# A mixture-of-experts kernel after an mLSTM: the second expert's matrices requested later, its first matrix cast and split later

## The chip, the cores and the metric

The kernel runs on one core of a Trainium2 chip. The metric is the device time of one execution in microseconds. The engines are called PE (TensorE, matrix products), ACT (ScalarE), DVE (VectorE), POOL (GpSimd) and SP (SyncE, which here only issues transfers). "SPq" is SP's sequencer. Transfers that SP issues share one queue on the 16 DMA engines; indirect transfers (gathers and scatters) are issued by POOL on another.

## The reference

The first stage is a recurrent attention with a matrix state for 4 sequences of 768 steps and 8 heads of 40; its result, scaled by a sigmoid gate, makes 3072 rows `x` of 320 numbers. The second stage is a mixture of 16 experts (4 groups of 4), and each row goes to one of them:

```python
g_idx = np.argmax(x @ w_group, axis=1)              # the group, g_w its softmax weight
e_idx = np.argmax(xg @ w_expert[g], axis=1)         # the expert in it, e_w its softmax weight
h = np.maximum(xg[mask_e] @ w1[g, e], 0.0)          # 320 -> 1024
ye = h @ w2[g, e]                                   # 1024 -> 320
out[tok_idx] = (g_w * e_w)[:, None] * ye
```

## The kernel before

The whole order of instructions is written out by hand; each engine runs its own in program order, and the framework puts in the waits. The first stage goes through 24 units (6 chunks of 128 steps, 4 sequences). While it runs, every unit's rows are stored in the DRAM tensor `x_d`, the rows' experts are found, and a table `itab` in DRAM takes, expert by expert, the number and weight of each row (scatters by POOL).

The experts then run in order of falling size, each with room for a fixed number of rows (384 in the first, 352 in the second, and so on down). An expert has these steps. Its index list `ix` is loaded from `itab`; POOL gathers its rows (`xg`, in blocks of 128) from `x_d` by that list; PE transposes them (line 778), and ACT and DVE make of them a high and a low half (`xhl`). Its matrices are loaded as `w1s` (1536 KB) and `w2s` (1280 KB); ACT casts each piece to a high half and DVE makes the low half, the difference (`w1h`, `w1l`, `wsk`, `w2h`, `w2l`; lines 728 and 732). PE makes the first products in four groups `psh` (line 758), ACT and DVE make of each a high and low relu (`hh`), and PE makes the second products `po` (lines 803 to 805). ACT scales these to `y`, which POOL scatters to the output (line 615).

The first expert is begun before all rows are known. Its first 256 rows (the early block, `early_expert`, lines 685 to 718) are gathered while the last units run. Its last 128 rows (the late block) are those that came from the last chunk: they don't go by the index list. POOL scatters the last chunk's rows straight into a small DRAM tensor `x_l` (`put_places`, line 513), and SP loads this as `xg` (line 1311); the load must wait for all scatters. PE transposes the rows in `early_turn` (line 675), called in the middle of the early block's second group of 128 rows, between its sixth and seventh of eight filter rows. The late block is narrow: its groups hold 256 columns (high and low together), and ACT copies a part `hs` (line 863) and DVE adds the rest (line 864) before the relu.

The order around the change:

- `last_units` (line 995) ends the first stage. After the last store it issues, on SP, a tiny transfer `peek` that waits for the early gathers (line 1113), and then `do(early_loads)` (line 1114). `early_loads` holds what is left of the requests for the first two experts' matrices: at this place the second expert's four, two halves of `w1s` and two of `w2s` (`load_tasks`, line 624).
- `lists` (line 1307) is a generator whose pieces run between the early block's groups of first products. Its first piece puts the last rows into `x_l`, requests the load of `x_l` on SP, scatters the last rows' numbers to `itab`, and requests on SP the late rows' list `li` (line 985) and the second expert's `ix` (line 644). `li` waits for the scatters into `itab`. The next piece requests the third expert's list and lets POOL gather the second expert's rows (`load_x`, line 611).
- `early_expert` calls `after()` between its first and its second products. Before the change this is `second_w1`, which casts and splits the second expert's `w1` (three casts on ACT, three differences on DVE).
- `expert((0, 1), ...)` (line 1340) runs the late block. Its argument `own` is a list of casts; after each of the four groups of first products one of them is taken, cast and split. Before the change the list is empty. In the middle of the late block's second products PE transposes the second expert's rows (`turn2`, through `mid`, line 799).
- The second expert then runs in the loop from line 1344, with the casts of its `w2` as `own`.

Of the kernel before, what the change touches and what calls it, by code (L numbers as in the profile page):

```python
# [42 lines left out]
NEARLY, NPICK, EARLY, LATE = 1, 2, 256, 128  # L43
CAPS = [EARLY + LATE, 352, 320, 288, 256, 256, 256, 256, 192, 192, 192, 192, 160, 160, 160, 128]
# [12 lines left out]
def lstm_moe(ctx: ExitStack, tc: tile.TileContext, gates, qkT, nat, og, wcat, w1, w2, cst, out):  # L57
# [38 lines left out]
    ps_1 = first_banks.enter_context(tc.tile_pool(name="ps_1", bufs=1, space=PSUM))  # L96
# [21 lines left out]
    rt = {}  # L118
# [370 lines left out]
    def put_id():  # L489
        if ids:  # L490
            sl, tk = ids.pop(0)
            nc.gpsimd.memset(sep, 0.0)
            no_order("ids", nc.gpsimd.indirect_dma_start(
                out=itab_flat, out_offset=bass.IndirectOffsetOnAxis(ap=sl, axis=0), in_=tk, in_offset=None))


    def put_ids():
        while ids:
            put_id()
# [118 lines left out]
    ereg, w1st, w2st, ixs, wsp_, xhls = {}, {}, {}, {}, {}, {}  # L618
# [66 lines left out]
    def early_expert(W, ws, idx, lists, after, last):  # L685
        w1h, w1l, wsk, w2h, w2l = (ws[n] for n in ("w1h", "w1l", "wsk", "w2h", "w2l"))
        xhl = xhls[0, 0]
        hh = pools["hp"].tile([P, NF, 2 * W], F32R, name="hh")
        xh, xl = [xhl[:, k, 0, :] for k in range(3)], [xhl[:, k, 1, :] for k in range(3)]
        for f in range(0, NF, 2):  # L690
            ps = pools["ps_h"].tile([P, 512], F32, name="psh")
            for g in range(2):
                s0 = slice((f + g) * P, (f + g + 1) * P)
                s1 = slice(F + (f + g) * P, F + (f + g + 1) * P)
                todo = [(w1h, s0, xh[0]), (w1h, s0, xl[0]), (w1h, s1, xh[1]), (w1h, s1, xl[1]), (wsk, s0, xh[2]),
                        (wsk, s0, xl[2]), (w1l, s0, xh[0]), (w1l, s1, xh[1])]
                for n, (w, s, x) in enumerate(todo):
                    mm(ps[:, g * W:(g + 1) * W], w[:, s], x, start=(n == 0), stop=(n == len(todo) - 1))
            if f == 0:
                steps(lists)  # L700
            a, hr = ps.rearrange("p (q w) -> p q w", q=2), hh[:, f:f + 2, 0:W]
            nc.scalar.activation(hr, a, AF.Relu)
            nc.vector.scalar_tensor_tensor(hh[:, f:f + 2, W:], a, 0.0, hr.bitcast(F32), op0=ALU.max, op1=ALU.subtract)
            steps(lists)
        after()
        for i, m in enumerate(blocks(W)):
            t, tl = slice(i * P, i * P + m), slice(W + i * P, W + i * P + m)
            po = pools["ps_o"].tile([P, DM], F32, name="po")
            for f in range(NF):
                s = slice(f * DM, (f + 1) * DM)  # L710
                if f == NF - 2 and i == len(blocks(W)) - 1:
                    do(last())
                mm(po, hh[:, f, t], w2h[:, s], start=(f == 0), stop=False)
                mm(po, hh[:, f, t], w2l[:, s], start=False, stop=False)
                mm(po, hh[:, f, tl], w2h[:, s], start=False, stop=(f == NF - 1))
            y = pools["hp"].tile([P, DM], F32, name="y", bufs=3)
            nc.scalar.activation(y, po, AF.Copy, scale=idx(i, m)[:, 1:2].bitcast(F32))
            no_order("out", scatter(y, idx(i, m)[:, 0:1]))
# [197 lines left out]
    def do(tasks, n=99):  # L916
        while tasks and n:
            tasks.pop(0)()
            n -= 1

    def ix_of(r):
        return lambda i, m: ixs[r][0:m, i, :]

    xgs, early_loads, early_splits = {}, [], []
# [54 lines left out]
    def steps(g, n=1):  # L979
        for _ in range(n):  # L980
            next(g, None)
# [13 lines left out]
    def last_units():  # L995
        a, b, c, d = range(HAND, NU)
        loads(d)
        decays(c, "upper")
        put_ids()
        decays(d, "upper")  # L1000
        scores(a)
        norm(a - 1)
        norm1(a - 1)
        norm2(a - 1)
        norm3(a - 1, "reciprocal")
        masked(a, 0)
        norm3(a - 1, "mult")
        masked(a, 1)
        carried(a)
        rows(a - 1)  # L1010
        logits(a - 2)
        carried2(a)
        turn(a - 1)
        r1 = turned_logits(NCH - 2)
        steps(r1, 2)
        values(a)
        steps(r1, 4)
        decays(c, "exp")
        steps(r1)
        logits(a - 1)  # L1020
        r2 = route(NCH - 2, B - 1, B, rt["bank"])
        steps(r1, 2)
        norm(a)
        steps(r1)
        norm1(a)
        steps(r1)
        norm2(a)
        steps(r1)
        norm3(a, "reciprocal")
        steps(r1, 4)  # L1030
        put_ids()

        scores(b)
        steps(r2)
        steps(r1)
        steps(r2)
        steps(r1)
        steps(r2, 2)
        masked(b, 0)
        steps(r2, 2)  # L1040
        masked(b, 1)
        carried(b)
        steps(r2)
        decays(d, "exp")
        steps(r2)
        norm3(a, "mult")
        steps(r2)
        carried2(b)
        steps(r2, 2)
        rows(a)  # L1050
        steps(r2, 6)
        put_ids()
        load_ix(0, nc.gpsimd)
        xgs[0] = load_x(EARLY, ix_of(0), True)
        steps(r2, 2)
        steps(early_counts(), 9)
        values(b)

        turn(a)
        late_first()  # L1060
        do(early_splits, 2)
        scores(c)
        norm(b)
        norm1(b)
        norm2(b)
        norm3(b, "reciprocal")
        masked(c, 0)
        norm3(b, "mult")
        masked(c, 1)
        logits(a)  # L1070
        carried(c)
        rows(b)
        carried2(c)
        values(c)
        do(early_splits)
        do(lows, 2)

        turn(b)
        scores(d)
        norm(c)  # L1080
        norm1(c)
        norm2(c)
        norm3(c, "reciprocal")
        masked(d, 0)
        norm3(c, "mult")
        masked(d, 1)
        logits(b)
        r3 = route(NCH - 1, 0, 2, rt["bank"])
        carried(d)
        steps(r3, 2)  # L1090
        rows(c)
        steps(r3, 3)
        carried2(d)
        steps(r3)
        values(d)
        steps(r3)
        busy(1)
        turn(c)
        busy(2)
        norm(d)  # L1100
        steps(r3)
        norm1(d)
        steps(r3)
        norm2(d)
        steps(r3)
        norm3(d, "reciprocal")
        steps(r3)
        norm3(d, "mult")
        steps(r3)
        rows(d)  # L1110
        logits(c)
        turn(d)
        nc.sync.dma_start(peek, xgs[0][-1][0:1, 0:2])
        do(early_loads)
        xl = early_turn((0, 0), EARLY, xgs[0], ((ps_a, "it"), (ps_s, "sp")))
        steps(r3, 9)
        put_rows()
        put_ids()
        put_places(late_p, xgs["late"])
        do(lows, 1)  # L1120
        do(xl)
        logits(d)
        busy(4)
        rt["r4"] = route(NCH - 1, 2, B, rt["bank"])
        steps(rt["r4"], 6)
# [29 lines left out]
    with tc.manual_schedule():  # L1155
# [106 lines left out]
        tp = gate_cols(1, NCH)  # L1262
# [40 lines left out]
        own, rest = casts(1)  # L1303
# [3 lines left out]
        def lists():  # L1307
            steps(rt["r4"], 12)
            put_rows()
            xgs[0, 1] = [mxp.tile([P, ROW], F32, name="xg", bufs=8)]  # L1310
            nc.sync.dma_start(xgs[0, 1][0][0:LATE], x_l)
            put_ids()
            li = late_list()
            rt["late"] = lambda i, m: li[0:m]
            load_ix(1)
            yield
            next(experts)
            load_e(2, [ET.SP, ET.Pool])
            load_ix(2)
            xgs[1] = load_x(CAPS[1], ix_of(1))  # L1320
            yield
            do(lows, 1)
            yield
            do(lows, 2)
            yield

        def second_w1():
            for act, low in own:
                act()
                low()  # L1330

        early_expert(EARLY, wsp_[0], ix_of(0), lists(), second_w1, lambda: early_turn((0, 1), LATE, xgs[0, 1], [(ps_1, "tp")]))
        load_w1(2, nc.gpsimd)
        load_w2(2, nc.gpsimd)
        early_banks.close()
# [1 line left out]
        pools["ps_h"] = enter(tc.tile_pool(name="ps_h2", bufs=3, space=PSUM, reuse_waits="tile"))  # L1337
        pools["ps_o"] = enter(tc.tile_pool(name="ps_o2", bufs=2, space=PSUM, reuse_waits="tile"))
        pools["late"] = True
        expert((0, 1), LATE, rt["late"], [], (), lambda: turn2(1, CAPS[1], xgs[1]))  # L1340
        own = rest
        next(experts, None)
        xgs[2] = load_x(CAPS[2], ix_of(2))
        for r in range(NEARLY, NE):
# [12 lines left out]
            own = list(rest)  # L1357
# [3 lines left out]
    with tc.For_i(0, nv, 1):  # L1361
# [31 lines left out]
        tp = pools["ps_h"].tile([P, 2, 512], F32, name="psh")[:, 0, 0:3 * P].rearrange("p (k w) -> p k w", k=3)  # L1393
# [83 lines left out]
```

## Time and profile before

| | us |
|---|---|
| median of 3 runs | 434.77 |
| lowest and highest | 433.32, 435.80 |
| the profiled execution | 429.81 |
| its span in the trace | 427.8 |
| PE busy | 393.3 (92% of the span) |
| DVE busy | 326.5 (76%) |
| ACT busy | 273.4 (64%) |
| POOL busy | 194.6 (45%) |
| DMA, mean over the span | 221 GB/s |

A busy engine is one that executes; register, branch and DMA-issuing instructions don't count. In a timeline each line is start, duration (both in us), engine, line of the kernel, operation, output and inputs, count, and in brackets how long the engine was idle before and what ended that. In a list of waits the numbers are the total, the count and the longest. In the chain of waits each line is start, duration and what the end was waiting for at that time. In windows the columns are the stretch, its length, the busy time of PE, of PE's weight load, DVE, ACT and POOL, then the clock granted to PE as a share of full speed, the share of time in which the DMA engines were busy, and GB/s. `psh`, `po` and the like are the program's tiles; `a<-b,c` is an instruction that writes a and reads b and c.

### The profile page before, as it was taken

What the parts mean: (1) busy time and instruction counts of PE and PEld (TensorE: products, weight loads), DVE (VectorE), ACT (ScalarE), POOL (GpSimd) and SP (SyncE); (2) the same over time, 40 slices, a digit from 0 to 9 for tenths busy, and PEclk for the clock granted to TensorE, in tenths of its full rate; (3) what the DMA queues carried; (4) which work ended last, traced back from release to release, by engine and by line L of the source; (5) the groups of instructions that cost most, each with busy time, mean ns of one, the idle gap of its engine ahead of it and who ended that gap; (6) DMA issues with size and microseconds to landing.
All of it is one profiled execution on the core that took longest, in us unless ns stands there. A gap on an engine that the chain in (4) does not pass through costs nothing.

```text
span 427.8 us, 9374 instructions
## 1 busy us (share of the span) xinstructions
PE 393.3 (92%) x3341; PEld 374.2 (87%) x3341; DVE 326.5 (76%) x738; ACT 273.4 (64%) x607; POOL 194.6 (45%) x220
## 2 busy tenths in 40 slices
PE   8888999897988898979999999999999999999960
PEld 5878989887977797969999999999999999999960
DVE  5787898989879899747837465666669999999940
ACT  3858677585778733444745466567468888888840
POOL 6656576774857626546231322422422334442210
PEclk9999999999999999999999999999999999999995
DMA  6969998998999616639864657657665877676000
GB/s 186 296 181 329 314 314 255 268 280 230 311 332 308 160 40 180 197 83 338 314 220 133 216 199 254 202 188 276 209 227 211 317 264 246 229 274 243 2 25 1
DMA packets 30518, 94.73 MB, mean 221 GB/s; under 512 B 9600, under 2 KB 13953, under 8 KB 26886
## 3 DMA queue, kind: packets, MB, share of 16 engines
q1 hardware_dynamic: 25094, 79.48, 57.8%
q0 software_dynamic: 5104, 14.28, 9.6%
q8 instruction: 27, 0.44, 0.4%
q10 hardware_dynamic: 272, 0.36, 0.3%
q14 instruction: 21, 0.17, 0.2%
HBM read 83.84 MB, written 12.00 MB: 224 GB/s over the span
## 4 chain that ended last, share of the span: by engine, by line
PE 58%; DVE 11%; DMA 10%; ACT 8%; issue 6%; POOL 4%; POOLq 0%; SPq 0%; DVEq 0%; ACTq 0%
PE psh L758 24%; PE po L803 6%; PE po L804 6%; PE po L805 6%; ACT ab L191 3%; PE psh L778 2%; DMA x_d<-x 2%; PE po L809 2%; PE sp L201 2%; PE po L808 2%; PE av L277 2%; DMA ab<-a_d 2%; DVE pt L207 2%; DMA qk<-in_qkT_dram 1%; PE busy L125 1%
## 5 line engine op out<-in xcount | busy, mean ns | idle before, releaser
L615 POOL DMA_INDIRECT out_dram<-y,ix x34 | 44.9, 1320 | 132.8 <-ACT y L817 115.4
L758 PE MATMUL psh<-xhl,w1h 128*128 128x256 f32 (+4 forms) x368 | 85.8, 309 | 0.4 <-DVE xhl L678 0.3
L758 PEld LDWEIGHTS psh<-xhl,w1h 128*128 128x128 f32 x368 | 59.9, 189 | 1.0 <-DVE xhl L678 0.5
L803 PE MATMUL po<-w2h,hh 128*128 128x320 f32 (+1 forms) x192 | 60.7, 316 | 0.0
L804 PE MATMUL po<-w2l,hh 128*128 128x320 f32 (+1 forms) x192 | 59.3, 309 | 0.0
L805 PE MATMUL po<-w2h,hh 128*128 128x320 f32 (+1 forms) x192 | 59.2, 308 | 0.0
L191 ACT ACTIVATE ab<-ab,bcol 128x128 f32<-128x128 f32 x176 | 53.8, 388 | 4.5 <-POOL ab L158 2.9
L732 DVE TENSOR_TENSOR w2l<-w2s,w2h 128x640 fp32r<-128x640 f32 x64 | 51.8, 824 | 6.3 <-ACT w2h L728 5.3
L277 PE MATMUL av<-nt,pt 128*128 128x128 f32 x384 | 49.4, 282 | 1.9 <-DVE pt L207 1.9
L758 PE MATMUL psh<-xhl,w1l 128*128 128x256 f32 (+6 forms) x256 | 49.1, 273 | 0.0
L277 PEld LDWEIGHTS av<-nt,pt 128*128 128x128 f32 x384 | 45.0, 192 | 3.3 <-DVE pt L207 1.7
L201 PE MATMUL sp<-qk 128*128 128x128 f32 x384 | 47.0, 276 | 0.0
L758 PE MATMUL psh<-xhl,wsk 128*128 128x256 f32 (+4 forms) x184 | 46.8, 304 | 0.0
L853 DVE SCALAR_TENSOR_TENSOR hh<-psh,hh 128x512 fp32r<-128x512 f32 (+3 forms) x36 | 21.5, 615 | 32.2 <-ACT hh L850 32.0
L611 POOL DMA_INDIRECT xg<-x_d,ix x34 | 35.8, 1053 | 21.6 <-DMA ix<-itab 11.3
L728 ACT CAST w2h<-w2s 128x640 fp32r<-128x640 f32 x64 | 44.9, 723 | 0.0
L201 PEld LDWEIGHTS sp<-qk 128*128 128x128 f32 x384 | 44.8, 192 | 0.2
L732 DVE TENSOR_TENSOR w1l<-w1s,w1h 128x1024 fp32r<-128x1024 f32 x32 | 38.9, 1219 | 6.4 <-ACT w1h L728 6.2
L758 PEld LDWEIGHTS psh<-xhl,w1l 128*128 128x128 f32 x256 | 42.4, 188 | 0.0
L850 ACT ACTIVATE hh<-psh 128x512 fp32r<-128x512 f32 (+3 forms) x28 | 18.0, 644 | 31.9 <-PE psh L758 31.9
L207 DVE TENSOR_TENSOR pt<-sp,ab 128x512 f32<-128x512 f32 x48 | 32.7, 683 | 4.7 <-PE sp L201 2.8
L803 PEld LDWEIGHTS po<-w2h,hh 128*128 128x128 f32 (+1 forms) x192 | 35.8, 187 | 0.5
(200 smaller groups left out, 872.7 us busy)
## 6 DMA issues: line engine op xcount, KB each, us to landing
w1s<-in_w_dram SPq DMA_DIRECT2D x12, 1536.0 KB
w2s<-in_w_dram SPq DMA_DIRECT2D x13, 1280.0 KB
ab<-a_d SPq DMA_DIRECT2D x22, 512.0 KB
nt<-in_nat_dram SPq DMA_DIRECT2D x24, 324.0 KB
qk<-in_qkT_dram SPq DMA_DIRECT2D x48, 160.0 KB
x_d<-x SPq DMA_DIRECT2D x23, 192.0 KB
sig<-in_og_dram SPq DMA_DIRECT2D x6, 640.0 KB
w1s<-in_w_dram SPq DMA_DIRECT2D x4, 768.0 KB
```

Of the source, the lines that this page charges most:

```text
L191: nc.scalar.activation(ab[:, j, :], ab[:, j, :], AF.Exp, bias=bcol[:, c, b * H + j:b * H + j + 1])
L201: mm(sp[:, jj, :], qk[:, j % 2, j // 2, :], qk[:, 2, j // 2, :], start=True, stop=True)
L207: nc.vector.tensor_tensor(pt, t["pm"][hh], t["ab"][:, 4 * hh:4 * hh + 4, :], op=ALU.mult)
L277: mm(t["av"][:, o:o + P], t["pm"][hh][:, jj, :], nt[:, o:o + P], start=True, stop=True)
L611: return nc.gpsimd.indirect_dma_start(out=o, out_offset=None, in_=src, in_offset=bass.IndirectOffsetOnAxis(ap=idx, axis=0))
L615: return nc.gpsimd.indirect_dma_start(out=out, out_offset=bass.IndirectOffsetOnAxis(ap=idx, axis=0), in_=y, in_offset=None, bounds_check=N ...
L728: nc.scalar.copy(t[names[0]][:, dst], src[r][:, s])
L732: nc.vector.tensor_tensor(o, src[r][rows, s], h.bitcast(F32), op=ALU.subtract)
L758: mm(ps[:, g, 0:n_], w[:, s], x, start=(n == 0), stop=(n == len(todo) - 1))
L803: mm(po[0:m], hh[:, f, t], w2h[:, s], start=st0, stop=False)
L804: mm(po[0:m], hh[:, f, t], w2l[:, s], start=False, stop=False)
L805: mm(po[0:m], hh[:, f, tl], w2h[:, s], start=False, stop=sp0)
```

## The change

The second expert's four requests go from the end of the first stage to the first piece of `lists`, right behind the request for the load of `x_l` and ahead of those for `li` and `ix`, on the same queue. `early_expert` gets nothing to do between its products, and the late block gets the three casts and splits as `own`: the first three of its four groups are each followed by one.

```diff
@@ last_units
         turn(d)
         nc.sync.dma_start(peek, xgs[0][-1][0:1, 0:2])
-        do(early_loads)
         xl = early_turn((0, 0), EARLY, xgs[0], ((ps_a, "it"), (ps_s, "sp")))
@@ lists
             put_rows()
             xgs[0, 1] = [mxp.tile([P, ROW], F32, name="xg", bufs=8)]
             nc.sync.dma_start(xgs[0, 1][0][0:LATE], x_l)
+            do(early_loads)
             put_ids()
             li = late_list()
             rt["late"] = lambda i, m: li[0:m]
             load_ix(1)
@@
-        def second_w1():
-            for act, low in own:
-                act()
-                low()
-
-        early_expert(EARLY, wsp_[0], ix_of(0), lists(), second_w1, lambda: early_turn((0, 1), LATE, xgs[0, 1], [(ps_1, "tp")]))
+        early_expert(EARLY, wsp_[0], ix_of(0), lists(), lambda: None, lambda: early_turn((0, 1), LATE, xgs[0, 1], [(ps_1, "tp")]))
         load_w1(2, nc.gpsimd)
         load_w2(2, nc.gpsimd)
@@
-        expert((0, 1), LATE, rt["late"], [], (), lambda: turn2(1, CAPS[1], xgs[1]))
+        expert((0, 1), LATE, rt["late"], list(own), (), lambda: turn2(1, CAPS[1], xgs[1]))
         own = rest
```

## The prediction

> **What bounds the kernel now.** I read the page first, then the waits of the tensor engine (PE), the chain of waits around the one large wait, and then the engines' timelines there.
>
> ```profile
> span 427.8 us, 9374 instructions
> ```
>
> The waits of PE over the whole span, and those after 196 us (in total, times, longest):
>
> ```profile
> PE tpm L675 <- DMA xg<-x_l: 2.6, 1, 2.6
> ...
> PE psh L758 <- DVE xhl L786: 0.2, 1, 0.2
> ```
>
> The first is the largest single wait of PE for a transfer in the span: it wants the late block's rows, `xg<-x_l`. The second is all that PE waits for between 196 and 412 us. So from the second expert on, PE is the bound, and whatever makes that expert start later or earlier moves the end by as much. The change has to be judged by one number: when the second expert's first products can run.
>
> The chain of waits from 174 to 187 us:
>
> ```profile
> 174.66 4.47 DMA x_l<-pt,place
> ...
> 179.15 5.68 DMA xg<-x_l
> ...
> 184.87 0.56 PE tpm L675 x3
> ...
> 186.58 0.45 PE psh L758 x2
> ```
>
> The last scatter into `x_l` lands at 174.66 + 4.47 = 179.13, its load takes 5.68 more, and PE transposes at 184.87. PE's timeline beside it:
>
> ```profile
> 181.93 0.31 PE L715 MATMUL po<-w2h,hh 128*128 128x320 f32 x1
> ...
> 193.04 1.07 PE L778 MATMUL psh<-cs,xg 128*128 128x128 f32 x9
> ...
> 196.22 0.75 PE L758 MATMUL psh<-xhl,w1h 128*128 128x352 f32 x3 [0.17 <-DVE xhl L786]
> ```
>
> PE runs out of work at 182.24 and stands for 2.63 us. The late block's products begin at 186.58 (T below); at 193.04, which is T + 6.46, stand the transposes of the second expert's rows, and 3.18 later, at 196.22, its products run without gaps. **The most that the change can win is that stall of 2.63 us, 0.6% of the run.**
>
> **The part that is moved: four requests on SP's queue.** SP's timeline:
>
> ```profile
> 166.49 0.90 SPq L629 DMA_DIRECT2D w1s<-in_w_dram  x2
> ...
> 167.57 1.41 SPq L629 DMA_DIRECT2D w2s<-in_w_dram  x2
> ...
> 179.15 0.33 SPq L1311 DMA_DIRECT2D xg<-x_l  x1
> 183.06 0.33 SPq L985 DMA_DIRECT2D li<-itab  x1
> 183.58 2.37 SPq L644 DMA_DIRECT2D ix<-itab  x3
> ```
>
> The matrices (two halves of w1 of 768 KB, two of w2 of 640 KB, 2.88 MB) are issued from 166.49 to 168.98. Moved behind the load at 179.15, they have nothing before them on SP but that load. Behind them come `li` and the index lists `ix`. SP is done with four requests 2.5 us after it starts, before `li` may go (it waits for the last scatter into `itab`), so SP itself holds up nothing. The queue of the transfers does.
>
> **What it wins: scatters.** The gather queue's timeline (POOL):
>
> ```profile
> 172.06 1.00 POOL L513 DMA_INDIRECT x_l<-xg,late_p  x1 [0.30 <-issue]
> ...
> 176.55 1.00 POOL L493 DMA_INDIRECT itab<-tokw,slot  x1 [0.25 <-issue]
> ...
> 186.24 0.97 POOL L611 DMA_INDIRECT xg<-x_d,ix  x1 [7.43 <-DMA ix<-itab]
> ...
> 188.78 0.93 POOL L611 DMA_INDIRECT xg<-x_d,ix  x1 [0.30 <-issue]
> ```
>
> And the time from issue to landing of three of these, those at 172.06, 176.55 and 188.78, in this order:
>
> ```profile
> DMA to landing us min/median/max: 6.7/6.7/6.7
> ...
> DMA to landing us min/median/max: 3.0/3.0/3.0
> ...
> DMA to landing us min/median/max: 3.2/3.2/3.2
> ```
>
> DMA in windows of one microsecond (the last two columns are the share of the 16 engines and GB/s):
>
> ```profile
> 174.00:175.00 1.00, 1.00 (x11) 1.00 (x10) 1.00 (x3) 0.60 (x1) 0.70 (x2) 1.00 1.02 412
> ...
> 176.00:177.00 1.00, 1.00 (x9) 1.00 (x8) 0.97 (x2) 0.60 (x1) 0.75 (x3) 1.00 0.31 109
> ```
>
> The matrices keep the engines full at 412 GB/s and are through at about 176.5, 10.0 us after the first request. A scatter beside them takes 6.7, one just behind them 3.0. POOL issues its scatters 1.3 apart whatever the DMA does, so the last still goes out at 174.66; with 3.0 in place of 4.47 it lands at 177.7, 1.45 earlier (bounds: 0 and 1.45). The load's 5.68 was taken with the engines almost idle; I leave it (bounds from the landings above: 3.2, as a gather of 128 such rows takes, to 6.7). Rows land at 183.4; PE stands 1.2 instead of 2.63, and T becomes 185.1.
>
> **What it costs: the index lists of the second expert.** The place in the queue matters, and a later part of the trace shows it. SP, then POOL:
>
> ```profile
> 349.39 0.33 SPq L629 DMA_DIRECT2D w2s<-in_w_dram  x1
> 350.36 0.38 SPq L644 DMA_DIRECT2D ix<-itab  x1
> ```
>
> ```profile
> 358.25 1.22 POOL L611 DMA_INDIRECT xg<-x_d,ix  x1 [1.49 <-DMA ix<-itab]
> ```
>
> An `ix` of 2 KB, issued a microsecond behind a matrix of 1280 KB, is still waited for 7.9 us after its issue. At 183.58, with nothing ahead, `ix` let POOL gather at 186.24, 2.66 after its issue. So small loads on SP's queue come behind the matrices ahead of them. Here 2.88 MB stand ahead, issued from 178.0. Three ways to place their end: at 412 GB/s from the request, 7.0 us, 185.0; at the pace of the same four requests now, 10.0 us, 188.0; at 412 GB/s but only once the rows of `x_l`, ahead of them in the same queue, are in at 183.4, 190.4. The lists take their 2.66 behind that: 187.7, 190.7 or 193.1, against 186.24. I take 191.3: the 10.0 us are of the same transfers, and had no slow load ahead of them, so somewhat more.
>
> Three gathers follow: the third goes out 2.54 behind the first (186.24 to 188.78) and lands 3.2 later. Now that is 191.98, 1.06 before the transposes want it. After: 191.3 + 2.54 + 3.2 = 197.0. The transposes stand in the middle of the late block's second products, in PE's order, so PE stands there until 197.0, and the second expert runs 3.18 later, at 200.2 instead of 196.22: **4.0 us later**. Bounds by the other two ends: 187.7 gives 193.4 and 196.6 (+0.4), 193.1 gives 198.8 and 202.0 (+5.8).
>
> **The other part: cast and split.** ACT, then DVE, now and in the late block, and PE's first second-product of that block:
>
> ```profile
> 179.20 2.00 ACT L728 CAST w1h<-w1s 128x1024 fp32r<-128x1024 f32 x2 [2.49 <-DMA x_l<-pt,place]
> ```
>
> ```profile
> 180.28 2.36 DVE L732 TENSOR_TENSOR w1l<-w1s,w1h 128x1024 fp32r<-128x1024 f32 x2 [2.85 <-ACT w1h L728]
> 182.68 1.22 DVE L732 TENSOR_TENSOR wsk<-w1s,wsk 64x1024 fp32r<-64x1024 f32 x1
> ...
> 188.44 0.42 DVE L864 TENSOR_TENSOR hs<-hs,psh 128x256 f32<-128x256 f32 x1 [1.91 <-ACT hs L863]
> ```
>
> ```profile
> 191.27 0.31 PE L803 MATMUL po<-w2h,hh 128*128 128x320 f32 x1
> ```
>
> Six instructions leave 179.2 to 183.9. That wins nothing: PE ran its own products then, and only a y behind them comes sooner. They go between the late block's groups, which PE makes in 1.17 us each (186.58 to 191.27 over four), while DVE then has 0.42 + 0.42 + 1.22 = 2.06 per group. In DVE's order from T + 1.86 (188.44): add, a split that waits for its 1.0 us cast and ends at T + 4.1, then add, relu, split, add, relu, some 0.08 overlapped at each, to T + 6.6. PE wants that second relu's low half at T + 5.9 (191.27 is T + 4.69, two filter rows of 0.44 and two matmuls later). So +0.7 to the transposes' natural time: T + 7.2 = 192.3. And PE then waits for the gathers until 197.0 anyway: these 0.7 cost nothing unless the gathers are early (bounds 0 and, with all three splits on the path, 3.7). The casts find their matrix: T + 1.7 = 186.8 is behind the first half even if w1 comes last in its share. Behind the lists on POOL's queue stand two scatters of y and the third expert's matrices; these shift by the same few microseconds, and so does the stage that wants them.
>
> **Sum.** -1.45 for the scatters, all of it swallowed by the new wait; +4.0 for the second expert's start. The profiled execution took 429.81 (span 427.8), 1.1% under the median of 434.77; 4.0 makes 433.8 of it, and **438.8** of the median.
>
> **The rivals.**
>
> *The clock falls in the new wait.* PE would stand 197.0 - 192.3 = 4.7 us. The granted clock (PEclk, third column from the end) in two windows, and PE's last matmul:
>
> ```profile
> 182.00:187.00 5.00, 2.09 (x15) 1.58 (x13) 2.42 (x3) 1.58 (x4) 0.76 (x1) 1.00 0.26 35
> ...
> 415.00:416.00 1.00, 0.00 (x0) 0.00 (x0) 0.00 (x0) 0.00 (x0) 0.06 (x1) 0.88 0.23 81
> ```
>
> ```profile
> 412.93 0.31 PE L805 MATMUL po<-w2h,hh 128*128 128x320 f32 x1
> ```
>
> The stall of 2.63 kept the full clock; after the last matmul (413.24) the clock is seen falling within 3 us. So 4.7 us may be enough. The price: eleven matmuls at the start, from cold, against four later ones of the same line:
>
> ```profile
> 1.27 4.88 PE busy L125 x11
> ```
>
> ```profile
> 167.20 1.04 PE L125 MATMUL busy<-ones_b 128*128 128x512 bf16 x4
> ```
>
> 0.44 each against some 0.22: 4.9 us at half pace lose 2.4. I estimate that some 0.4 of it lies beside the casts and splits that the second expert's start waits for in any case (the 0.17 at 196.22 is what is seen of that wait now). That is +2.0, or 440.8. [...]
>
> *The transfer is hidden anyway.* The matrices go through at full pace from their request, so the lists are ready by 186.6 and the gathers by 192.3. Then the new wait is gone, T is 1.45 earlier, and the 0.7 on DVE, and 0.1 to 0.2 behind it, come back on the path: second expert 0.6 earlier, 434.2; up to the first end above, +0.4, 435.2. For it: 412 GB/s is shown. Against: the four requests took 10.0 us, not 7.0, and here they queue behind a load of 5.68. With the load of `x_l` at 3.2 as well, PE never stands and it reaches -1.8.
>
> *The scatters are no faster.* Their landing stays at 179.13, and all of it, lists too, comes 1.45 later: +5.5, 440.3. Against: 6.7 beside the matrices, 3.0 without.
>
> **How the numbers follow.** Forecast 0.40, clock 0.33, hidden 0.20, scatters 0.07. About 0.5% (2.2 us) is what a measurement of this kernel can tell from no change. Slower: the forecast without a tenth of it that lies under 2.2, the clock and the scatters, 0.36 + 0.33 + 0.07 = 0.76. Faster needs more than the hidden case's own figure: 0.04 of it. Same: 0.20. The range goes from the hidden case's upper end, 435.2, to the forecast's bound of +5.8 with most of the clock's 2.0, 442.4; what is left out is half of the hidden case and the corner where list and clock are both at their worst.
>
> **What would show it.** Right: `x_l` scatters land in about 3 us; POOL's wait for `ix` before the second expert's gathers ends near 191; PE's largest wait is at the transposes of line 778, some 4 to 5 us; the wait at line 675 is about 1.2; PE after that waits for nothing. The clock's case shows as PEclk under 1.00 around 197 to 202. Wrong: if the gathers still go out by 187, or if PE waits instead for a cast (`w1h`, line 728) whose matrix came late.

## The result and the profile after

The changed kernel takes 438.09 us in the median of 4 runs (437.75 to 442.4), the kernel before 434.04 beside it (433.16 to 435.8). The ratio is 1.0118, with an interval of 1.0069 to 1.0168: 1.2% slower, 5.1 us, between 3.0 and 7.3 (the two medians are 4.05 apart). The profiled execution took 438.38.

The page after, its span and the row of the granted clock in 40 slices:

```profile
span 436.4 us, 9373 instructions
...
PEclk9999999999999999996999999999999999999995
```

Before, that row was full from the first slice to the last but one. Now one slice in the middle is at 6. The waits of PE, in total, times and longest:

```profile
PE psh L778 <- DMA xg<-x_d,ix: 3.3, 3, 1.6
...
PE po L805 <- DVE hh L853: 0.5, 1, 0.5
```

The wait for the late block's rows at line 675 (2.6 before) is gone from the list. In its place PE waits at line 778 for the second expert's gathers, three times, once for each block of rows. The 0.5 at line 805 is the late block's low relu behind a split on DVE.

SP's timeline, then POOL's:

```profile
178.81 0.34 SPq L1310 DMA_DIRECT2D xg<-x_l  x1
179.38 0.85 SPq L629 DMA_DIRECT2D w1s<-in_w_dram  x2
180.42 1.88 SPq L629 DMA_DIRECT2D w2s<-in_w_dram  x2
186.86 0.33 SPq L985 DMA_DIRECT2D li<-itab  x1
187.38 2.37 SPq L644 DMA_DIRECT2D ix<-itab  x3
```

```profile
176.62 0.99 POOL L513 DMA_INDIRECT x_l<-pt,place  x1 [0.30 <-issue]
...
179.19 0.98 POOL L493 DMA_INDIRECT itab<-tokw,slot  x1 [0.22 <-issue]
194.43 0.98 POOL L611 DMA_INDIRECT xg<-x_d,ix  x1 [14.27 <-DMA ix<-itab]
195.72 1.51 POOL L611 DMA_INDIRECT xg<-x_d,ix  x1 [0.31 <-issue]
197.53 1.02 POOL L611 DMA_INDIRECT xg<-x_d,ix  x1 [0.30 <-issue]
```

POOL stands 14.27 us for the list, where it stood 7.43. The chain of waits tells what that time was made of:

```profile
179.19 7.66 DMA itab<-tokw,slot
...
187.38 6.24 DMA ix<-itab
```

There are two holds and not one. The last scatter into `itab` takes 7.66 to land (177.85 to 183.06 before, 5.2), and SP's `li` and `ix` wait for it; and the list takes 6.24, so that POOL gathers 7.05 after its issue, where it had gathered 2.66 after it. The list lands only when the matrices are through. In windows of one microsecond:

```profile
189.00:190.00 1.00, 1.00 (x11) 1.00 (x10) 0.00 (x0) 0.00 (x0) 0.00 (x0) 1.00 1.01 391
190.00:191.00 1.00, 1.00 (x11) 1.00 (x10) 0.42 (x1) 0.91 (x2) 0.00 (x0) 1.00 0.80 80
```

The bulk ends at about 190.2, 10.8 after its first request at 179.38, and the gathers begin 4.2 behind that. PE and the clock behind that:

```profile
195.74 0.31 PE L805 MATMUL po<-w2h,hh 128*128 128x320 f32 x1
197.60 0.55 PE L778 MATMUL psh<-cs,xg 128*128 128x128 f32 x3 [1.56 <-DMA xg<-x_d,ix]
...
204.56 0.92 PE L758 MATMUL psh<-xhl,w1h 128*128 128x352 f32 x4
```

```profile
197.00:198.00 1.00, 0.40 (x3) 0.31 (x3) 0.60 (x2) 0.29 (x1) 0.69 (x2) 0.98 0.11 26
198.00:199.00 1.00, 0.15 (x2) 0.00 (x0) 0.00 (x0) 0.00 (x0) 0.69 (x2) 0.50 0.58 174
...
204.00:205.00 1.00, 1.00 (x6) 1.00 (x6) 0.92 (x3) 0.20 (x1) 0.00 (x0) 0.61 0.79 270
```

PE runs dry at 196.05, and from 198.0 to 204.8 it has half its clock: through the rest of the transposes, the late block's last products and into the second expert's first. Those products begin at 204.56, against 195.74 before; 2.0 of that is the stage's later place in this execution. Behind them nothing changes: from there to the end of the span it is 231.8 us, and 232.1 before.

The first stage differs by several microseconds between executions of one and the same kernel (the last scatter into `x_l` goes out at 174.66 in the first profile of before and at 185.37 in the second), and so do whole spans (427.8 and 438.5). So below I count from a mark inside the stage, the issue of the last scatter into `x_l` (174.66 before, 176.62 after). The expectations count from the early block's first product; the two marks stand 6.7 to 8.0 us apart in the fourteen profiles, so a difference of a microsecond depends on which one is taken. From the scatter, the two profiles of before agree on the second expert's start to 0.1. Where an expectation speaks of the second expert's products, it means the start of their run without gaps, 0.3 to 1.1 behind the first product of the table. All numbers are differences of starts in the timelines of one execution each:

| kernel | `x_l` load requested | `li` requested | first gather | second expert's first product | clock halved in the wait | time over before (95%) |
|---|---|---|---|---|---|---|
| before | 4.5 | 8.4 | 11.6 | 21.1 | no | |
| before_again | 4.1 | 7.4 | 10.7 | 21.0 | no | |
| changed | 2.2 | 10.2 | 17.8 | 27.9 | yes | 1.0118 (1.0069 to 1.0168) |
| after_again | 2.2 | 12.1 | 17.2 | 27.0 | yes | 1.0100 (1.003 to 1.017) |
| casts_only | 2.2 | 7.2 | 11.7 | 20.9 | no | 1.0038 (0.9994 to 1.0081) |
| loads_only | 2.2 | 12.3 | 17.4 | 29.2 | yes | one execution only |
| half_moved | 2.2 | 10.4 | 13.7 | 22.7 | yes | 1.0012 (0.9979 to 1.0045) |
| behind_li | 2.2 | 7.4 | 19.4 | 28.9 | yes | one execution only |
| behind_list | 2.2 | 7.8 | 12.0 | 23.1 | yes | 1.0067 (1.003 to 1.0103) |
| ix_by_pool | 2.2 | 11.5 | 16.4 | 25.8 | yes | 1.0106 (1.0026 to 1.0186) |
| kept_busy | 2.2 | 11.3 | 16.8 | 25.4 | no | 1.0064 (1.0022 to 1.0107) |
| pool_and_busy | 2.2 | 11.6 | 16.6 | 25.0 | no | 1.0121 (1.0051 to 1.0192) |
| w2_behind_list | 2.2 | 7.5 | 11.9 | 20.3 | no | 1.0007 (0.9969 to 1.0045) |
| asked_early | 2.2 | 7.7 | 11.8 | 20.3 | no | 1.0165 (1.0117 to 1.0214) |

By this count the change costs 6.4 us (27.5 against 21.0, means of two before rounding), which is 1.5% and inside the interval of the times. From the early block's first product it is 7.0. Each ratio is to runs of before on the same chip.

### The profile page after: what moved, and what is told of

The parts are those of the page before. It is cut to its first block, busy times and chain, and to the rows that moved or that the text cites. A ratio compares the mean times of both kernels' runs of the same rounds, so it can differ in the third digit from the quotient of the medians.

```text
span 436.4 us, 9373 instructions
## 1 busy us (share of the span) xinstructions
PE 398.8 (91%) x3341; PEld 376.9 (86%) x3341; DVE 326.9 (75%) x738; ACT 273.1 (63%) x607; POOL 194.9 (45%) x220
## 4 chain that ended last, share of the span: by engine, by line
PE 51%; ACT 11%; POOL 10%; DVE 9%; issue 8%; DMA 6%; POOLq 0%; SPq 0%; another core or an unknown queue 0%; DVEq 0%; ACTq 0%
PE psh L758 22%; PE po L803 6%; PE po L804 6%; PE po L805 6%; ACT ab L191 5%; POOL ab L158 3%; DMA itab<-tokw,slot 3%; PE psh L778 2%; PE po L809 2%; POOL kw L214 2%; POOL itab L493 2%; PE po L808 2%; DVE pt L207 2%; DMA ix<-itab 1%; ACT L188 1%
## 5 line engine op out<-in xcount | busy, mean ns | idle before, releaser
L803 PE MATMUL po<-w2h,hh 128*128 128x320 f32 (+1 forms) x192 | 61.4, 320 | 0.0
L805 PE MATMUL po<-w2h,hh 128*128 128x320 f32 (+1 forms) x192 | 60.0, 312 | 0.5 <-DVE hh L853 0.5
```

The lines of the kernel that those rows point to most:

```text
L803: mm(po[0:m], hh[:, f, t], w2h[:, s], start=st0, stop=False)
L805: mm(po[0:m], hh[:, f, tl], w2h[:, s], start=False, stop=sp0)
```

## The experiments

**The two kernels once more.** No edit.

> The changed kernel once more, for a second profile and for times beside its variants. Both theories: about 4 us over before (0.9%). The list theory (the second expert's index list queues behind the matrices) expects that POOL waits for the list until 192 to 195, PE waits at the transposes of line 778 for 3 to 5 us, and the granted clock falls there. In the first profile ACT and DVE also waited up to 5 us for PE between 171 and 183, with no releaser that the profile knows; if that comes from the change it is there again, if it is chance of one execution it is not.

> The kernel before once more, for a second profile. Counted from the first product of the early block, the second expert's products ran at 28.3 us in the first profile of before, at 36.0 and 35.4 in the two of the changed kernel. If that difference is the change's, this profile gives 27 to 30; if it was chance of executions, up to 33. Its scatters into x_l may land faster than the 4.5 to 7.1 of the first profile, if the matrices happen to be through sooner.

The second profile of the changed kernel has the same long wait of POOL (here with the one of the first expert in it), and the halved clock:

```profile
POOL xg L611 <- DMA ix<-itab: 15.7, 2, 13.5
```

```profile
202.00:204.00 2.00, 1.07 (x4) 0.70 (x5) 0.00 (x0) 0.00 (x0) 1.70 (x2) 0.50 0.53 154
```

There the two holds are split otherwise than in the first:

```profile
184.42 9.38 DMA itab<-tokw,slot
...
194.34 3.84 DMA ix<-itab
```

The scatter takes longer and the list less, 13.2 together where they were 13.9, and the end is in the same place: the matrices are through at about 195.2, 10.7 after their first request, and the gathers go out 3.8 behind that. Its time is 1.0100 of before. A wait in the first profile, of ACT, had no releaser that the trace knows:

```profile
ACT hh L702 <- remote: 8.3, 2, 5.3
```

In the second profile ACT's waits at that line (8.6 in all, the longest 4.5) are for PE's products, and none is without a releaser, so nothing ties this wait to the change (`half_moved` has one of 2.4). The late block's transposes began at 10.3 by the table's count in the first profile and at 8.2 in the second, but the second expert was held by its gathers in both. The second profile of before gives 21.0 to the first's 21.1, and its scatters land little faster (4.1 to 4.5), with PE waiting less:

```profile
PE tpm L675 <- DMA xg<-x_l: 1.5, 1, 1.5
```

So what there was to win at that place was 1.5 us in one execution and 2.6 in the other.

**Each half of the change alone.**

```diff
 # casts_only: before, with
-        early_expert(..., lists(), second_w1, ...)
+        early_expert(..., lists(), lambda: None, ...)
-        expert((0, 1), LATE, rt["late"], [], (), ...)
+        expert((0, 1), LATE, rt["late"], list(own), (), ...)
```

> The kernel before with the cast and split of the second expert's first matrix between the late block's groups, as in the change, but the matrices requested where they were. List theory: DVE's row of work delays the second expert by 0.7 to 0.9 us, no more: at most 0.3% over before. Rival, that the casts on the late block's path are the loss: 3 to 5 us over before.

```diff
 # loads_only: before, with
-        do(early_loads)                                   # in last_units
             nc.sync.dma_start(xgs[0, 1][0][0:LATE], x_l)
+            do(early_loads)
```

> The first half of the change alone: requests moved as in the change, casts left ahead of the early block's second products. The casts then wait on ACT for their matrix (requested 10 after the early block's first product, in at 18 to 21), and the late block's own cast stands behind them: its products at 21 to 23 instead of 17.6 to 19.8. The second expert is held by its gathers (25) in any case: products at 36 to 38, no better than the whole change, 0 to 2 worse.

PE's waits of the first:

```profile
PE psh L778 <- DMA xg<-x_d,ix: 2.3, 2, 1.4
...
PE po L805 <- DVE hh L853: 0.5, 1, 0.5
```

The casts cost a wait of 0.5 at the late block's relu and no more; the second expert begins at 20.9, as before, and the time is 1.0038 with an interval that holds 1. The casts on the late block's path are not the loss. With the requests moved alone, ACT and PE show:

```profile
193.77 1.04 ACT L728 CAST w1h<-w1s 128x1024 fp32r<-128x1024 f32 x1 [6.63 <-DMA w1s<-in_w_dram]
197.49 1.04 ACT L728 CAST w1h<-w1s 128x1024 fp32r<-128x1024 f32 x1 [2.68 <-DMA w1s<-in_w_dram]
```

```profile
PE psh L758 <- DVE xhl L678: 7.8, 1, 7.8
```

The casts stand on ACT for their matrix, the late block's `xhl` stands behind them, and PE waits 7.8 us for it. It ends worse than the whole change, 29.2 to 27.5, with the same gathers (17.4). The expectation had the right size with a wrong reason: it took the second expert to be held by its gathers in any case, and here PE comes to the transposes at 210.84 without waiting for them, held by the late cast alone. So moving the casts is what makes the moved requests bearable, and the moved requests are what costs.

**How many bytes are moved.**

```diff
 # half_moved: before, with
-        do(early_loads)                                   # in last_units
+        do(early_loads, 2)                                # w1 only
             nc.sync.dma_start(xgs[0, 1][0][0:LATE], x_l)
+            do(early_loads)                               # w2
```

> The kernel before, its casts of w1 where they were, with only the two halves of w2 (1.31 MB of the 2.88) moved behind the load of x_l. Counted from the early block's first product, the gathers of the second expert went out at 18.4 in both profiles of before and at 25.0 to 25.6 in those of the changed kernel. Theory, that the matrices in flight hold the list back by their bytes: about 45% of these 7, gathers at 21 to 22, second expert's products at 30 to 31 (28.3 to 29.2 before, 35.4 to 36.0 changed), and no or a short fall of the clock. Rival, that any request ahead of the list costs the whole wait: gathers at 25.

The gathers go out at 13.7, 2.5 after before, where the whole change has 6.4: 40% of the wait for 45% of the bytes. In the expectation's own count they stand at 21.7, in its 21 to 22; the second expert's products at 31.7, somewhat over its 30 to 31, for the clock fell here too, for half as long (its mean is 0.87 from 200 to 205 and 0.79 from 205 to 210, some 3.4 us at half, where the changed kernel has 6.8). In the table that is 1.7 over before, and the time shows no difference beyond its interval. A request ahead of the list does not cost the whole wait; the wait goes with the bytes in flight, as far as one size between and one execution of it show.

**Which of the two holds.** Three places for the requests or the list:

```diff
 # behind_li: changed, with
-            do(early_loads)
             put_ids()
             li = late_list()
+            do(early_loads)
```

> The changed kernel, but the matrices are requested behind li and ahead of ix. li waits for the last scatter into itab, so the scatters run free of the matrices and only the list's queueing behind them is left. Queue theory alone: li is issued 15 us after the early block's first product as before, ix 18, and it lands behind the 10 us of matrices, gathers at 26 to 27 (25 in the changed kernel): no gain. If the scatters into itab, slowed by the matrices, were the larger part, the gathers come at 21 to 22.

```diff
 # behind_list: changed, with
-            do(early_loads)
             put_ids()
             ...
             load_ix(1)
+            do(early_loads)
```

> The changed kernel, but the matrices are requested behind li and ix of the second expert. Neither scatters nor list then meet the matrices: both theories expect ix issued 15 to 16 us after the early block's first product and the gathers 18 to 19, as before. The casts of w1 then wait for their matrix, requested at 16 and landed at 21 to 25, and hold up the late block: second expert's products at 30 to 32, against 35 to 36 in the changed kernel and 28 in before; 3 to 4 us faster than the changed kernel, 2 slower than before.

```diff
 # ix_by_pool: changed, with
-            load_ix(1)
+            load_ix(1, nc.gpsimd)
```

> The changed kernel, but the second expert's index list is requested by POOL, on POOL's own queue, and not by SP behind the matrices. List theory: the gathers go out about 3 us after the last scatter into itab lands, not behind the matrices: 4 to 5 us earlier than in the changed kernel, the wait of PE is nearly gone and with it the fall of the clock; 3 to 5 us faster than the changed kernel, within 1 us of before. Rival, that the scatters into itab, slowed by the matrices, are what comes late (their landing took 7.7 where it was 5.2): only the 6.2 of the list's own way goes down to 3, 2 us faster at most. Rival, that the casts on DVE cost it: no faster.

SP and POOL of `behind_li`:

```profile
194.38 0.35 SPq L985 DMA_DIRECT2D li<-itab  x1
...
199.04 2.48 SPq L644 DMA_DIRECT2D ix<-itab  x3
```

```profile
206.41 0.98 POOL L611 DMA_INDIRECT xg<-x_d,ix  x1 [15.69 <-DMA ix<-itab]
```

Here the scatters run free (`li` at 7.4, as in before_again), and the list, issued 4.7 behind `li`, is waited for another 7.4. The gathers come at 19.4, later than in the changed kernel: the place behind the matrices, without slowed scatters, is enough for the whole loss. Of it, some 4 us are SP's own: it issues the four requests between `li` and `ix`, which stood 0.5 apart before; the rest is the longer wait behind the issue, 7.4 where it was 2.7. POOL of `ix_by_pool`:

```profile
189.31 0.79 POOL L644 DMA_DIRECT2D ix<-itab  x1 [8.04 <-DMA itab<-tokw,slot]
193.94 1.00 POOL L611 DMA_INDIRECT xg<-x_d,ix  x1 [3.84 <-DMA ix<-itab]
```

Here the list doesn't queue behind the matrices, and POOL waits 8.04 for the scatter instead, then 3.84 for the list. The gathers come only 1.1 earlier than in the changed kernel (16.4 to 17.5), the second expert 1.7, and the time, 1.0106, isn't better. The list theory expected 4 to 5 us and is wrong in this form. What came is the rival named there: the scatters beside the matrices are late too. Not even the 1.1 need be POOL's queue, since `kept_busy`, with the list on SP, has its first gather at 16.8. The holds lie side by side, and taking away one leaves the other. What the executions have in common is the end of the matrices: by windows of one microsecond, the first gather goes out 2.0 to 4.2 us behind it in all eight that have matrices ahead of or beside the list (changed, after_again, loads_only, half_moved, behind_li, ix_by_pool, kept_busy, pool_and_busy), on either queue. Whether the list and the scatters are held by the order in a queue or by engines that are shared is not separated by these runs. With neither hold, in `behind_list`, the gathers go out at 12.0, but the casts now wait:

```profile
196.37 1.05 ACT L728 CAST w1h<-w1s 128x1024 fp32r<-128x1024 f32 x1 [2.26 <-DMA w1s<-in_w_dram]
```

The second expert comes at 23.1, 2.0 over before and 4.4 under the changed kernel, and the time is 1.0067: as expected in both theories.

**The clock.**

```diff
 # kept_busy: changed, in turn2, at the second expert's first tile
+                    if r == 1 and i == 0:
+                        for _ in range(14):
+                            mm(tp[:, 1, :], ones_b, bc(ones_b.unsqueeze(1), (P, 4, P)), start=True, stop=True)
```

> The changed kernel with fourteen products of ones (128x512, bf16, some 3 us in all) on PE just ahead of the transposes of the second expert's rows; their results are overwritten. If the fall of the clock costs about 2 us of the loss, the granted clock stays at 1.00 and the run is 1.5 to 2.5 us faster than the changed kernel. If the clock is not the cause, no change, or slower by the part of the 3 us that outlasts the wait (0 to 1).

`pool_and_busy` has this edit and that of `ix_by_pool`.

> Both remedies in the changed kernel: the list requested by POOL, and the fourteen products ahead of the transposes. With the list by POOL the second expert's products ran at 33.3 after the early block's first, with the products at 32.7, without both at 35.4 to 36.0. If the two losses are separate (list held in the queue some 2, clock some 1.5), together 31.5 to 32. If each remedy only removed what the other would have, 32.7 to 33.3 again. What is left over before (28.3 to 29.2) is then the scatters into itab, whose landing the matrices slow.

PE of `kept_busy`, and its clock in the window behind the wait:

```profile
200.13 3.19 PE L775 MATMUL psh<-ones_b 128*128 128x512 bf16 x14
203.55 0.55 PE L781 MATMUL psh<-cs,xg 128*128 128x128 f32 x3 [0.23 <-DMA xg<-x_d,ix]
```

```profile
206.00:208.00 2.00, 1.67 (x13) 1.70 (x14) 1.47 (x4) 0.90 (x3) 1.86 (x3) 1.00 0.42 151
```

The products fill 3.19 us of the wait, and the clock stays. From the issue of the third gather to the second expert's first product it is 7.0, 6.9, 6.9 and 6.9 in the four executions with a halved clock and all three blocks late (changed, after_again, ix_by_pool, behind_li), with 3.1 to 3.3 of it from the issue to the third block's transposes, and 5.3 and 5.3 in the two that were kept busy, with 3.2 of it to the transposes: the clock costs 1.6, all of it behind them. In time, `kept_busy` has 1.0064 to the 1.0100 of the changed kernel beside it; the intervals overlap, so that step rests on the traces. `pool_and_busy` was to reach 31.5 to 32 if the two losses add up, and came to 33.4 in the expectation's count, a miss. By the table it is the earliest of the three, 25.0 to the 25.4 of `kept_busy` and the 25.8 of `ix_by_pool`. The 1.6 of the clock is there again, but the gathers went out at 16.6, where `kept_busy` without POOL's queue has 16.8. So the account by sums holds for the clock, and of the list's queue no gain of its own is shown.

**Versions meant to be better.**

```diff
 # w2_behind_list: before, with
-        do(early_loads)                                   # in last_units
+        do(early_loads, 2)                                # w1 only
             ...
             load_ix(1)
+            do(early_loads)                               # w2
```

> The kernel before with w1's two halves where they were and w2's two behind the second expert's list. Half the bytes beside the scatters into x_l, none ahead of the list: scatters land in 2 to 3 where they took 4.5, the load of x_l goes out at 10 instead of 11.3 to 11.8 after the early block's first product, gathers at 18.4 or a little later, w2 lands by 30, before its casts. Second expert's products at 27.5 to 29: at most 1 us (0.25%) faster than before, so the same within what the times can tell. If the gathers suffer from w2 beside them, 29 to 31 and slower by 0.3%.

```diff
 # asked_early: before, with
         loads(d)                                          # at the head of last_units
+        do(early_loads)
         ...
-        do(early_loads)                                   # behind peek
```

> The kernel before, casts where they were, but the second expert's matrices are requested right behind the last unit's loads, some 20 us earlier, where DMA is mostly idle. Scatters, x_l and list then meet no matrix: x_l's load is requested about 10 us after the early block's first product (11.3 before), PE's wait for it is 0 to 1.5 instead of 2.6, gathers go out at 18 as before. Expected: second expert's products at 27, 1 us faster than before, at most 0.5% in time. If the last units' stores queue behind the matrices instead, the early block begins later and it is 1 to 3 us slower.

With w2 behind the list the second expert begins at 20.3, 0.7 under before, and the time is 1.0007 (0.9969 to 1.0045): no difference that can be measured. Asked early, this stage is as good, 20.3, but the kernel is 1.65% slower. POOL and PE show where, in the first stage:

```profile
169.21 0.81 POOL L644 DMA_DIRECT2D ix<-itab  x1 [14.03 <-DMA itab<-tokw,slot]
```

```profile
PE lg L401 <- DVE oh L396: 8.0, 3, 7.2
```

The matrices meet the earlier scatters into `itab` there: POOL waits 14.03 for them, where it waited 6.55 in the kernel before, and PE 7.2 behind a late store, where its longest wait at that line was 0.8. That is the case the expectation named last, at 1 to 3 us; it cost 7. The same hold, at another place. None of the versions beats the kernel before by more than can be told apart.

## Why the prediction was right, and where it fell short

*The mechanism.* Right: the wait for `x_l` goes and a longer one for the second expert's gathers takes its place, at the transposes of line 778. That it is the requests and not the casts is shown by `casts_only`; that it grows with the bytes, by `half_moved`; that the place behind the matrices suffices for it, by `behind_li`. The wait at line 778 was put at 4 to 5 us in one piece and was 3.3 and 4.3 in three.

*The scatters into `x_l`.* The direction was right and the gain larger: they land in 2.2 beside no matrix (3.0 taken); the load goes out 2.1 earlier by the count (1.45 taken). The wait at line 675, put at 1.2, is gone. All of it was swallowed, as said. In `casts_only` they land in 2.2 too, though the matrices were asked for at the old place: there the matrices were through by about 176.6 (DMA's busy share was 1.00 from 174 to 176, 0.34 from 176 to 178 and 0.06 from 178 to 180), and the last scatter was issued at 177.62. So even this gain isn't there in every execution.

*The list.* The direction was right, and the term was too small by about 1.3. The end of the matrices came as taken: 10.6 us behind their first request in the sum (188.6 less 178.0), 10.8 and 10.7 in the two profiles, from a request that went out some 0.6 earlier by the count. The step that was mis-sized is the one behind it: 2.66 from there to the first gather in the sum, 4.2 and 3.8 measured. The prediction held `li` to its old time, since "SP itself holds up nothing". But `li` waits for the scatters into `itab`, and these now run beside the matrices: `li` at 10.2 and 12.1 instead of 8.4 and 7.4, and `ix` stands behind it on SP. I had priced the matrices beside the scatters into `x_l` (6.7 against 3.0) and didn't ask which scatters they would meet at their new place. How much of the wait is the scatters' and how much the list's differs between the two profiles, and stays open; `behind_li` shows only that the second is enough in a kernel without the first. The first gather was put at 16.6 by the same count (191.3 less 174.66) and came at 17.8 and 17.2.

*The gathers.* Taken as one wait, they are three: PE transposes each block as it lands. The third set the end, as taken; 2.5 from the first issue to the third was 3.1 and 2.9.

*The casts.* Right: the row on DVE shows as a wait of 0.5 (0.7 taken), hidden by the gathers.

*The clock.* Given as a rival at 0.33 and priced at 2.0, over and above the forecast; it happened in both profiles of the changed kernel and costs 1.6. Its reason didn't hold: the prediction asked for one unbroken wait of 4.7 us, and in the first profile the clock fell after 1.55, where before it had outlasted 2.63. The runs don't show what decides whether a wait costs the clock, so the 0.33 was an estimate of mine. The sum: 4.0 taken for the second expert's start, 6.4 measured by the count. Of the 2.4 between them the third gather's issue has 1.3 (20.9 and 20.1 instead of 19.2) and the clock 1.7 in these two profiles; and 0.6 went the other way, since two of the three blocks are transposed before the third lands (5.3 from its issue to the first product, by the kernels kept busy, where 3.2 + 2.7 had been taken). The measured times, 5.1 (3.0 to 7.3), hold both the forecast and the clock's case; that the median came within 1 us of the forecast is partly luck, as the stage itself lost 6.4.

*What lies behind.* Right: from the second expert on nothing is made good, 231.8 and 232.1 us to the end.

## What to carry to other kernels

A transfer that is moved in a queue must be checked against every small transfer that is issued behind it and against every scatter that is in flight beside it: here 2.88 MB in front of a list of a few kilobytes cost more than their absence from an earlier place could win. A stall of PE that is bought off by such a move is worth at most its own length, so read first who waits for the next small transfer in that queue, and how much slack it has (here 1.1 us). And a wait of PE can cost more than its length: here the clock was at 0.50 for the 6.8 us from 198.0 to 204.8, which cost 1.6 us.

## What the runs showed of the hardware

The clock fell after a shorter unbroken wait than one that it withstood. In the changed kernel PE ran dry at 196.05, did three transposes (0.55 in all) at 197.60, and had half its clock from 198.0 (0.50 from 198 to 199); in the kernel before it stood still for 2.63 us, from 182.24 to 184.87, and the clock stayed at 1.00 (182 to 187). After the last matmul of before, which ends at 413.24, it stayed full until 415.76 and was at 0.50 from 416 on. By the windows, the clock was halved in the stage between the two experts for some 3.4 us in `half_moved` and `behind_list`, for 6.8 in the changed kernel, in `after_again`, `ix_by_pool` and `behind_li`, and for 10.2 in `loads_only`; `asked_early` has some 17 at half clock ahead of that stage, between 165 and 185. No run shows what decides when the clock falls, and for how long.

A scatter of a few bytes per row into `itab` took 7.7 and 9.4 us to land beside the matrices in the two profiles of the changed kernel, and was waited for 14.0 in `asked_early`; the two of before that were issued as the matrices ended (176.55) or behind them (177.85) took 3.0 and 5.2. The last scatter into `x_l`, with no matrix beside it, landed in 2.2 in `after_again` and `casts_only`, and in the changed kernel the load that waits for it went out 2.2 behind its issue.
